# Decode attention with an MLP gate on one core: first and last loads cut by partitions, 96 rows of w2 moved to ACT's DMA queue

## The chip, the core and the metric

One core of a Trainium2 chip runs the whole kernel. The metric is device microseconds for one execution; less is better. Times given as a median come from runs without the profiler; everything else comes from one execution under the hardware profiler, whose own time is given beside its span below.

## The reference

Two tokens (B = 2, one position each, D = 512). With `xn = layernorm(x)`:

```
q = (xn @ wq) as (B, 32 heads, 1, 128)
s = softmax(q . k_cache * 128**-0.5) . v_cache      # 8192 positions a head
s = s as (B, 1, 4096) @ wo
g = silu( gelu( layernorm(xn) @ w1 + b1 ) @ w2 + b2 )   # w1 (512, 1376), w2 (1376, 512)
out = x + s * g
```

All is float32. k_cache and v_cache have 268 MB each, wq and wo 8.4 MB each, w1 and w2 2.8 MB each.

## The kernel before

The 64 (token, head) pairs are worked off in N = 32 steps of two heads. In a step, partition p holds 64 positions of one head: a K tile is 128 partitions x 64 KB (8.4 MB), a V tile the same. There are two K buffers (`kpool`) and one V buffer (`vpool`).

- **Loads.** All large loads go through `load` (L60) and SyncE's queue, in program order. `load_k(n + 2)` stands at the end of step n, after the last reader of K tile n; `load_v(n)` stands in step n behind `weighted(n - 1)`, the last reader of the only V buffer. A load waits on SyncE until its buffer is free, and what stands behind it in SyncE's queue waits with it. Each DMA has one of eight completion semaphores in turn, and a DMA also waits until the earlier DMA with its semaphore has landed.
- **Start.** The MLP's weights and small tensors lie in `boot`, which takes the place of the V buffer; wq takes one of the K buffers. SyncE issues w1 (L98), the first 1280 rows of w2 (L99), w2's last 96 rows (L100), wq (L101) and K tile 0 in two halves. ScalarE (ACT) issues x (L96), b1 in two loads (L107, L108) and b2 (L109) on its own queue. Then layernorm twice (`layernorm`, L152 to L158), transposes (L165), `mlp` (L196: w1, then b1 at L202, gelu, L215: w2, L218: b2), q (`project_q`, L241; `gather_q`, L251; `queries`, L262). TensorE runs these in that order. Only then can VectorE begin step 0 (L279), SyncE issue K tile 1 (waits for L241, the last reader of wq) and V tile 0 (waits for the last reader of `boot`).
- **A step.** VectorE multiplies K by q in two halves (L279) and sums over the 128 elements (L284), takes maxima (L288, L297); ACT does exp (L312); TensorE does the weighted sum over V (`weighted`, L327) and gathers the result (L337, L350). `max_dve(n - 1)` and `exps(n - 1)` stand in step n, after its first multiplication; `weighted(n - 1)` and `load_v(n)` follow.
- **End.** The last V tile is loaded in five pieces (`PIECES`, in 128ths of a partition's positions), wo in five (`WO_PIECES`, in its 32 rows c of 128 partitions x 2 KB) into a freed K buffer. At the end, 8 matmul instructions a row c (L419) sum `on` times wo, and two VectorE operations (L423, L424) and two small DMAs (L427) finish.

Of the kernel before, what the change touches and what calls it, by code (L numbers as in the profile page):

```python
# [8 lines left out]
F32 = mybir.dt.float32  # L9
AF = mybir.ActivationFunctionType  # L10
# [3 lines left out]
EPS = 1e-5  # L14
# [5 lines left out]
def decode_kernel(ctx: ExitStack, tc: tile.TileContext, x, kc, vc, wq, wo, w1, b1, w2, b2, out):  # L20
    nc = tc.nc
    P = 128
    B, H, S, DH = kc.shape
# [15 lines left out]
    NF = F // P  # L39
    FT = F - NF * P  # L40
    PH = P // H
    OC = DH // PH
    ZP = P - U * PH

    consts = ctx.enter_context(tc.tile_pool(name="consts", bufs=1))
    kpool = ctx.enter_context(tc.tile_pool(name="kpool", bufs=2))
    vpool = ctx.enter_context(tc.tile_pool(name="vpool", bufs=1))
    small = ctx.enter_context(tc.tile_pool(name="small", bufs=2))
# [9 lines left out]
    def load(dst, src, cuts):  # L58
        for a, e in zip(cuts, cuts[1:]):
            nc.sync.dma_start(dst[:, a:e], src[:, a:e])  # L60
# [5 lines left out]
    def load_v(n, cuts=(0, KP), pool=vpool, tag="v"):  # L66
        V[n] = pool.tile([P, KP, DH], F32, tag=tag, name=f"v{n}")
        load(V[n], vf[n], cuts)


    PIECES = (0, 32, 64, 96, 112, 128)
    WO_PIECES = (0, 8, 16, 24, 30, 32)


    wq_sb = kpool.tile([P, ND, H * DH], F32, tag="k", name="wq_sb")
# [3 lines left out]
    def take(p, n):  # L79
        a = used[0]  # L80
        used[0] += n
        assert used[0] <= KP * DH
        return boot[:p, a:a + n]

    w1_sb = take(P, ND * F).rearrange("p (c f) -> p c f", f=F)
    w2_sb = take(P, (NF + 1) * D).rearrange("p (c n) -> p c n", n=D)
    x_sb = take(B, D)
# [5 lines left out]
    z = take(P, P)  # L93
    th = take(P, P)

    nc.scalar.dma_start(x_sb, x.rearrange("b s d -> (b s) d"))  # L96

    nc.sync.dma_start(w1_sb, w1.rearrange("(p c) f -> p c f", p=P))  # L98
    nc.sync.dma_start(w2_sb[:, :NF, :], w2[:NF * P, :].rearrange("(p c) n -> p c n", p=P))  # L99
    nc.sync.dma_start(w2_sb[:FT, NF, :], w2[NF * P:, :])  # L100
    nc.sync.dma_start(wq_sb, wq.rearrange("(p c) n -> p c n", p=P))  # L101
    load_k(0, (0, KP // 2, KP))


    b1_sb = consts.tile([P, NF + 1], F32, name="b1_sb")
    nc.vector.memset(b1_sb, 0.0)
    nc.scalar.dma_start(b1_sb[:, :NF], b1[:NF * P].rearrange("(p c) -> p c", p=P))  # L107
    nc.scalar.dma_start(b1_sb[:FT, NF:NF + 1], b1[NF * P:, None])  # L108
    nc.scalar.dma_start(b2_sb, b2[None, :])  # L109
# [5 lines left out]
    nc.vector.memset(ones, 1.0)  # L115
    srow = consts.tile([1, HP], F32, name="srow")
    nc.vector.memset(srow, SCALE)
    eps_t = consts.tile([B, 1], F32, name="eps_t")
    nc.vector.memset(eps_t, EPS)

    mod = consts.tile([P, R], F32, name="mod")

# [231 lines left out]
    for n in range(N):  # L354
# [11 lines left out]
        if 1 <= n < LATE - 1 or n >= LATE:  # L366
# [7 lines left out]
            elif n == N - 1:  # L374
                load_v(N - 1, PIECES)
        if n >= LATE:
# [22 lines left out]
            load_v(n)  # L399

    wo_sb = kpool.tile([P, OC, D], F32, tag="k", name="wo_sb")
    load(wo_sb, wo.rearrange("(p c) n -> p c n", p=P), WO_PIECES)

    n = N - 1
    max_dve(n)
# [49 lines left out]
```

## Time and profile before

| | us |
|---|---|
| median of 3 runs (1307.24 to 1308.63) | 1308.48 |
| the profiled execution, its own time | 1307.31 |
| span of its trace, first to last instruction | 1305.5 |
| VectorE busy | 1128.8 (86%) |
| TensorE matmul busy | 444.4 (34%) |
| ACT busy | 84.0 (6%) |
| DMA queue q1 (SyncE's), share of 16 DMA engines | 99.3% |

The share of a DMA queue is the time that its packets took, over 16 engines for the whole span. A busy VectorE does not say that VectorE sets the end: the chain of waits from the last instruction backwards passes through DMA for 50% of the span and through VectorE for 48%.

### The profile page before, as it was taken

The page shows a single profiled execution, that of the slowest core. Times are in us where ns is not written, and L with a number is a line of the kernel's source. Part 1 is how long each engine was busy: PE and PEld are TensorE (multiplying, and loading weights), DVE is VectorE, ACT ScalarE, POOL GpSimd, SP SyncE. Part 2 cuts the span into 40 slices and gives each one's busy share as a digit, 9 for nine tenths or more (in the row PEclk, how much of TensorE's full clock was granted, in tenths as well). Part 3 has the DMA queues.
Part 4 walks back from the last instruction along what each step waited for, and adds up shares of the span by engine and source line. Part 5 has one row for each costly group of instructions (what it writes and reads, how often), then busy time and mean ns, then how long its engine had stood idle before and what let it go on. Part 6 is the DMA issues. An engine that isn't in the chain of part 4 may idle for free.

```text
span 1305.5 us, 7374 instructions
## 1 busy us (share of the span) xinstructions
PE 444.4 (34%) x3258; PEld 173.2 (13%) x3258; DVE 1128.8 (86%) x261; ACT 84.0 (6%) x276; POOL 2.8 (0%) x12
## 2 busy tenths in 40 slices
PE   6403333322333322333322333331333332231266
PEld 6101111111111101111100101110111101110013
DVE  1499989888889988889988888988888988889980
ACT  1100000000000000000000000000000000000000
POOL 0000000000000000000000000000000000000000
PEclk9756666556666656666655666655666655665668
DMA  9999999999999999999999999999999999999998
GB/s 398 440 424 442 424 442 422 442 424 442 424 442 424 438 430 436 432 434 432 432 436 428 440 426 438 428 440 424 440 426 440 424 444 422 446 404 426 438 416 339
DMA packets 11509, 559.76 MB, mean 429 GB/s; under 512 B 1515, under 2 KB 1523, under 8 KB 1750
## 3 DMA queue, kind: packets, MB, share of 16 engines
q1 hardware_dynamic: 11208, 559.29, 99.3%
q8 instruction: 25, 0.41, 0.1%
q10 hardware_dynamic: 270, 0.01, 0.0%
q14 instruction: 6, 0.05, 0.0%
HBM read 559.30 MB, written 0.00 MB: 428 GB/s over the span
## 4 chain that ended last, share of the span: by engine, by line
DMA 50%; DVE 48%; PE 1%; ACT 0%; issue 0%; SPq 0%; DVEq 0%
DMA k<-in_A_k_cache_dram 45%; DVE k L279 24%; DVE sc L284 24%; DMA wq_sb<-in_A_wq_dram 3%; DMA wo_sb<-in_A_wo_dram 2%; PE pq L241 1%; DVE nm L297 0%; ACT boot L244 0%; PE acc L419 0%; PE pqa L251 0%; SPq L60 0%; PE pb L262 0%; DVE mx L288 0%; SPq L100 0%; SPq L99 0%
## 5 line engine op out<-in xcount | busy, mean ns | idle before, releaser
L279 DVE TENSOR_TENSOR k<-k,q 128x8192 f32<-128x8192 f32 x64 | 555.5, 8681 | 109.7 <-DMA k<-in_A_k_cache_dram 98.0
L284 DVE TENSOR_REDUCE sc<-k 128x64 f32<-128x8192 f32 x64 | 552.4, 8666 | 0.0
L327 PE MATMUL po<-v,pz 128*8 128x512 f32 x2048 | 295.6, 742 | 202.3 <-DMA v<-in_A_v_cache_dram 202.3
L305 PE MATMUL pn<-nm,srow 1*64 1x1 f32 x128 | 11.7, 246 | 336.4 <-DVE nm L297 336.4
L327 PEld LDWEIGHTS po<-v,pz 128*8 128x8 f32 x2048 | 57.2, 104 | 422.8 <-DMA v<-in_A_v_cache_dram 213.7
L292 PE MATMUL pm<-ident,mx 128*1 128x128 f32 x32 | 11.8, 369 | 222.0 <-DVE Z L342 164.2
L305 PEld LDWEIGHTS pn<-nm,srow 1*64 1x64 f32 x128 | 9.0, 193 | 340.6 <-DVE nm L297 340.5
L334 ACT COPY o<-po 128x512 f32<-128x512 f32 x32 | 18.8, 586 | 516.3 <-PE po L327 516.3
L307 ACT COPY bias<-pn 128x1 f32<-128x1 f32 x32 | 5.1, 160 | 583.2 <-PE pn L305 583.2
L337 PE MATMUL pt<-mod,o 128*128 128x2 f32 x256 | 33.7, 254 | 22.9 <-ACT o L334 22.9
L337 PEld LDWEIGHTS pt<-mod,o 128*128 128x128 f32 x256 | 31.0, 191 | 52.6 <-ACT o L334 52.6
L318 PE MATMUL OA<-ones,ZR 128*128 128x1 f32 x64 | 18.6, 359 | 51.8 <-ACT ZR L315 51.8
L292 PEld LDWEIGHTS pm<-ident,mx 128*1 128x1 f32 x32 | 2.5, 79 | 224.4 <-issue 189.2
L312 ACT ACTIVATE pz<-sc,bias 64x128 f32<-64x128 f32 x64 | 25.5, 399 | 1.4
L318 PEld LDWEIGHTS OA<-ones,ZR 128*128 128x128 f32 x64 | 15.8, 307 | 54.5 <-ACT ZR L315 54.5
L262 PE MATMUL pb<-q_all,ident 64*64 64x128 f32 x128 | 21.6, 438 | 0.3 <-ACT q_all L253 0.3
L342 DVE TENSOR_TENSOR Z<-blk,pt 128x8 f32<-128x8 f32 x32 | 4.9, 152 | 18.4 <-PE pt L337 18.4
L196 PE MATMUL ph<-yT,boot 128*128 128x2 f32 (+1 forms) x88 | 19.5, 359 | 0.8 <-DMA boot<-in_B_w_dram 0.8
L196 PEld LDWEIGHTS ph<-yT,boot 128*128 128x128 f32 (+1 forms) x88 | 19.4, 317 | 0.9 <-ACT yT L166 0.9
L202 DVE TENSOR_TENSOR gh<-ph,b_sb 128x22 f32<-128x22 f32 x1 | 0.2, 181 | 21.0 <-PE ph L196 21.0
L350 PE MATMUL OA<-mod,Z 128*128 128x32 f32 x64 | 15.3, 332 | 4.4 <-DVE Z L342 4.3
L350 PEld LDWEIGHTS OA<-mod,Z 128*128 128x128 f32 x64 | 15.7, 304 | 4.8 <-DVE Z L342 4.8
(81 smaller groups left out, 119.5 us busy)
## 6 DMA issues: line engine op xcount, KB each, us to landing
k<-in_A_k_cache_dram SPq DMA_DIRECT2D x2, 4096.0 KB, 46.9
v<-in_A_v_cache_dram SPq DMA_DIRECT2D x3, 2048.0 KB, 19.2
wo_sb<-in_A_wo_dram SPq DMA_DIRECT2D x3, 2048.0 KB, 22.1
boot<-in_B_w_dram SPq DMA_DIRECT2D x1, 2752.0 KB, 9.7
boot<-in_B_w_dram SPq DMA_DIRECT2D x1, 2560.0 KB, 15.9
v<-in_A_v_cache_dram SPq DMA_DIRECT2D x2, 1024.0 KB
wo_sb<-in_A_wo_dram SPq DMA_DIRECT2D x1, 1536.0 KB
wo_sb<-in_A_wo_dram SPq DMA_DIRECT2D x1, 512.0 KB, 29.5
```

Of the source, the lines that this page charges most:

```text
L196: nc.tensor.matmul(ph[:w.shape[1], f * B:(f + 1) * B], w, yT[:, c, :], start=(c == 0), stop=(c == ND - 1))
L262: nc.tensor.matmul(p[HP * s:HP * (s + 1), :], w, q_all, start=True, stop=True)
L279: nc.vector.tensor_tensor(out=k, in0=k, in1=qb, op=ALU.mult)
L284: nc.vector.tensor_reduce(out=SC[n][:, a:e], in_=K[n][:, a:e, :], axis=AX.X, op=ALU.add)
L292: nc.tensor.transpose(p[:1, :], MX[n], ident)
L305: nc.tensor.matmul(p[HP * s:HP * (s + 1), :1], srow, nm[:, s:s + 1], start=True, stop=True)
L312: nc.scalar.activation(PZ[n % 3][r, :, s, :], sc[r], AF.Exp, bias=bias[r], scale=SCALE, accum_out=rs[r])
L318: nc.tensor.matmul(OA[:, b, OC:], ZR[:, a:a + P], ones[:, :1], start=False, stop=False)
L327: nc.tensor.matmul(po[R * j:R * j + U * JW, :], pz[:, t].rearrange("p s j -> p (s j)"), v[:, t * JW:(t + 1) * JW, :].rearrange("p j d -> p ...
L334: nc.scalar.copy(o4, PO[n % 2])
L337: nc.tensor.matmul(PT[n][:, :U], o4[:, i * DH:(i + 1) * DH], mod[:, i:U * JW:JW], start=(i == 0), stop=(i == JW - 1))
L350: nc.tensor.matmul(OA[:, b, :OC], Z[:, a:a + P], mod, start=False, stop=(n == N - 1))
```

## The change

- w1 is loaded in two DMAs instead of one: partitions 0 to 15, then 16 to 127.
- w2's last 96 rows go over ACT's queue instead of SyncE's, directly behind x.
- ACT first runs a `Sqrt` on a constant (`warm`), and only then issues x, w2's last rows, b1 and b2. The memset of that constant moves to the head of VectorE's stream.
- The last V tile is loaded in two pieces instead of five.
- wo is loaded in pieces of 16, 10, 4 and 1 rows, and its last row in four DMAs by partitions: 4, 5, 7 and 112.

```diff
-    PIECES = (0, 32, 64, 96, 112, 128)
-    WO_PIECES = (0, 8, 16, 24, 30, 32)
+    PIECES = (0, 64, 128)
+    WO_PIECES = (0, 16, 26, 30, 31, 32)
+
+    WO_SPLIT = (0, 4, 9, 16, 128)
...
-    nc.scalar.dma_start(x_sb, x.rearrange("b s d -> (b s) d"))
-
-    nc.sync.dma_start(w1_sb, w1.rearrange("(p c) f -> p c f", p=P))
+    w1_v = w1.rearrange("(p c) f -> p c f", p=P)
+    for p0, p1 in ((0, 16), (16, P)):
+        nc.sync.dma_start(w1_sb[p0:p1], w1_v[p0:p1])
     nc.sync.dma_start(w2_sb[:, :NF, :], w2[:NF * P, :].rearrange("(p c) n -> p c n", p=P))
-    nc.sync.dma_start(w2_sb[:FT, NF, :], w2[NF * P:, :])
     nc.sync.dma_start(wq_sb, wq.rearrange("(p c) n -> p c n", p=P))
     load_k(0, (0, KP // 2, KP))
...
+    eps_t = consts.tile([B, 1], F32, name="eps_t")
+    nc.vector.memset(eps_t, EPS)
     b1_sb = consts.tile([P, NF + 1], F32, name="b1_sb")
     nc.vector.memset(b1_sb, 0.0)
+    warm = small.tile([B, 1], F32, tag="warm", name="warm", bufs=1)
+    nc.scalar.activation(warm, eps_t, AF.Sqrt)
+    nc.scalar.dma_start(x_sb, x.rearrange("b s d -> (b s) d"))
+    nc.scalar.dma_start(w2_sb[:FT, NF, :], w2[NF * P:, :])
     nc.scalar.dma_start(b1_sb[:, :NF], b1[:NF * P].rearrange("(p c) -> p c", p=P))
...
-    eps_t = consts.tile([B, 1], F32, name="eps_t")
-    nc.vector.memset(eps_t, EPS)
...
-    load(wo_sb, wo.rearrange("(p c) n -> p c n", p=P), WO_PIECES)
+    wo_v = wo.rearrange("(p c) n -> p c n", p=P)
+    load(wo_sb, wo_v, WO_PIECES[:-1])
+    for p0, p1 in zip(WO_SPLIT, WO_SPLIT[1:]):
+        nc.sync.dma_start(wo_sb[p0:p1, OC - 1], wo_v[p0:p1, OC - 1])
```

## The prediction

> **What bounds the kernel now.** I read first the page's DMA rows and its 40 slices, then the chain of waits at its end, then the timelines of the first 160 us and the last 10.
>
> ```profile
> DMA  9999999999999999999999999999999999999998
> GB/s 398 440 424 442 424 442 422 442 424 442 424 442 424 438 430 436 432 434 432 432 436 428 440 426 438 428 440 424 440 426 440 424 444 422 446 404 426 438 416 339
> ...
> q1 hardware_dynamic: 11208, 559.29, 99.3%
> ...
> q10 hardware_dynamic: 270, 0.01, 0.0%
> ```
>
> Every slice has busy DMA engines, and q1, SyncE's queue, fills 99.3% of them. So the DMA queue is the bound, although the chain puts half of the span on VectorE: it follows each K load back to the VectorE sum that freed its buffer, but K tile 3, issued at 119.21, lands 35.4 us later, and 8.4 MB take 19.4, so it stood 16 us in the queue. The time is then start of the first packet (1.75 us), bytes over rate, any gap in which the queue runs dry, and what follows the last byte. Only the first and last slices (398, 339 GB/s) leave something to gain. The end, in the timeline:
>
> ```profile
> 1296.12 1.93 PE L419 MATMUL acc<-wo_sb,on 128*2 128x128 f32 x64 [2.16 <-DMA wo_sb<-in_A_wo_dram]
> ...
> 1299.80 1.93 PE L419 MATMUL acc<-wo_sb,on 128*2 128x128 f32 x64 [1.75 <-DMA wo_sb<-in_A_wo_dram]
> 1301.80 0.29 DVE L423 TENSOR_TENSOR res<-acc,gate 128x128 f32<-128x128 f32 x1 [12.84 <-PE acc L419]
> ```
>
> Rows 24 to 31 of wo begin when rows 24 to 29 have landed (1299.76 by the trace's landing events); the last two rows land at 1301.0, just as TensorE gets to them, and it ends at 1301.73. The start, in the same view:
>
> ```profile
> 0.74 0.39 SPq L98 DMA_DIRECT2D boot<-in_B_w_dram  x1
> 0.74 0.54 ACTq L96 DMA_DIRECT2D boot<-in_A_x_dram  x1
> ...
> 1.33 0.37 ACTq L107 DMA_DIRECT2D b_sb<-in_B_b_dram  x1
> ...
> 4.29 1.28 ACT L156 ACT_TABLE_LOAD   x1
> ...
> 10.53 19.49 PE L196 MATMUL ph<-yT,boot 128*128 128x2 f32 x88 [0.84 <-DMA boot<-in_B_w_dram]
> 30.06 0.18 DVE L202 TENSOR_TENSOR gh<-ph,b_sb 128x22 f32<-128x22 f32 x1 [20.97 <-PE ph L196]
> ...
> 38.03 7.05 PE L241 MATMUL pq<-wq_sb,xnT 128*2 128x512 f32 x64 [1.48 <-DMA wq_sb<-in_A_wq_dram]
> ```
>
> b1 is wanted at 30.06, and TensorE has 1.48 us to spare before wq. These two decide below.
>
> **Part by part.**
>
> *End.* The piece with rows 26 to 29 ends where the old fourth piece did, 1299.76. TensorE does 32 instructions (1.93 us / 64 = 0.030 each, 0.97) to 1300.77, row 30 (lands about 1300.4) to 1301.0, and row 31 from its landing: 8 instructions, 7 x 0.026 + 0.27 for the last = 0.45, to 1301.5, so 0.23 sooner. The last row now waits for four semaphores: one wait on TensorE's sequencer took 0.05 (row of L419), up to 0.15. The split by partitions shifts one 2 KB row (0.08 us in the packets of w2's last rows) off most DMA engines and up to two onto four of them: -0.08 to +0.16 on the last landing. The end takes -0.15, bounds -0.3 and +0.2. The other new pieces lie in cover: the second half of V is wanted after 32 of 64 matmuls, at about 1282.0, and lands at 1281.4; rows 0 to 15 of wo land at 1291.2, are done (4.95) at 1296.2, and rows 16 to 25 land only then, at about 1297.3. Without that cover nothing is late by over 1 us. SyncE's last three DMAs wait for V landings (the last at 1281.4, by the changed program's semaphores), 18 us before their bytes are due.
>
> *First load.* In the packet records the 16 engines begin their first 22,016-byte row between 1.75 and 2.72 and need 1.52 us on the mean, 0.82 for later ones. If one row an engine makes all begin together, at most 0.28 + 0.70 = 0.98 is gained; if the latency is HBM's, nothing; a second DMA's issue (0.39) might leave a hole, +0.3. I take -0.3, nearer to nothing, as even the row that began last took 0.98.
> [...]
>
> *w2's last rows.* On q1 their 96 packets of 2 KB and the first wq packets behind them (2.75 us on the mean, later 2.42) cost about 0.9 + 0.33 us an engine, where the bytes alone need 0.45. Between w1's big packets they should cost 0.08 each, 0.5 in all: -0.5, bounds 0 and -0.7.
>
> *Table load.* It moves from 4.29 to the start; x is issued after 1.28 + 0.29, at about 2.35 instead of 0.74. Behind it ACT issues w2's rows, b1 and b2 (0.4 each), to 4.7.
>
> *The new wait.* ACT's queue q10 is served one packet, or one semaphore write, after each q1 packet on the same engine: b1's 40-byte packets stand in the records exactly at the ends of w1's packets, 0.82 us apart. And b1, issued at 1.33, got its first turn at 5.64, after four w1 rows. So turns are the currency. Per engine q10 now has 6 + 1 (w2's rows), 8 + 1 (b1), 6 + 1 (b1's tail) = 23 turns, two more on the engines with x. w2's rows arrive at about 3.9, during row 2 of w1, and by the same delay are served after row 5, at 6.55. From there q1 offers 4 packets of w1 and a semaphore, 8 + 1 of w2, 8 + 1 of wq: 23, the last at about 36.3, since a wq packet takes 2.42. With x's two turns, up to two half-size K packets (1.21) more: b1's tail lands between 37.4 and 38.6 (landing events come 0.45 after), not at 17.4. VectorE's L202 waits for it: 30.06 becomes about 38, L215 1.77 later, its 4.37 and L218's 0.40 end at 44.5, and L241 starts there instead of 38.03: delay D = 6.0 to 7.2, I take 6.6. b2 lands by 41, before L218. x lands at about 7.5, so L196 starts near 12.7 and ends near 32: covered by b1. Were q10 served at once, this cover would go and L196 still leave L241 within 1 us of its time.
>
> What does D cost? All of step 0 moves by D, and these issues with it:
>
> ```profile
> 84.31 0.33 SPq L60 DMA_DIRECT2D k<-in_A_k_cache_dram  x1
> ...
> 105.59 0.33 SPq L60 DMA_DIRECT2D v<-in_A_v_cache_dram  x1
> 119.21 0.33 SPq L60 DMA_DIRECT2D k<-in_A_k_cache_dram  x1
> ```
>
> A DMA needs 1.0 from issue to first packet (0.74 to 1.75) and some 0.9 more before it streams. K tile 1 (45.13) must stream when K tile 0 ends on the engines, 55.1 to 56.9: room for D = 8.1. K tile 2 (84.31) follows V tile 0, from 93.8: 7.6. V tile 1 (105.59) follows K tile 2, 113.2 to 115.5: room 5.7 on the earliest engine, 8.0 on the latest, 6.7 on the mean; 0.8 less, as the gains above bring the queue forward. K tile 3 (119.21, room 11) and all later ones have more. So D = 6.6 costs the mean engine 0.7, the latest nothing: I take +0.5, bounds 0 and +3.5 (two turns more).
>
> Sum: -0.15 - 0.3 - 0.5 + 0.5 = -0.45. Against the profiled time 1306.9; the median is 1.17 above that execution, so 1308.0.
>
> **The rivals.**
>
> *The delay is absorbed.* If q10 is served soon after its arrival, because b1's wait for four rows had another cause (DMAs issued just before it), w2's rows get three turns more and b1's tail lands by 33: D under 3, no gap: -0.95, 1307.5. For it: only one such delay is in the trace. Against it: the same delay on all 16 engines.
> [...] The records here show one 40-byte descriptor a turn.
>
> *The queue runs dry (slower).* Place: V tile 1 behind K tile 2. Price: 1 us for each us of D beyond 5.9. Two more turns lost, through a later x or an HBM stall, give D = 9.0, a loss of 3.1, and 1308.48 - 0.95 + 3.1 = 1310.6; from D = 9.5 it is slower by over 0.2%. For it: no cover but the queue's backlog, and wq packets make a lost turn cost 2.42. Against it: my count puts only the last turn into that region.
>
> *The engines' spread closes (faster).* The last engine lands at 1301.0, the mean of the 16 at 1299.6. If split and pieces took all 1.4 and the first load its 0.98: -0.3 - 1.4 - 0.98 - 0.5 = -3.2, 1305.3. Against it: the split moves 0.08 to 0.16 us.
>
> *It does nothing.* Both start gains are HBM latency that stays: 1308.5.
>
> **Numbers.** Forecast 0.50, absorbed 0.25, runs dry 0.11, spread closes 0.07, nothing 0.07. A change under 0.2% (2.6 us) can't be told from none here. Same: 0.50 + 0.25 + 0.07 = 0.82; slower 0.11; faster 0.07. The range runs from near the faster case, 1305.7, to the dry queue at D = 9.0, 1310.6.
>
> **What would show it.** x's BN statistics at 7 us or later, L202 near 38 released by the b1 DMA, L241 at 43 to 46, V tile 1 issued at 111 to 113; wq's first packets at 2.42; TensorE's last row from 1301. Wrong if L202 stays near 32 (turns miscounted) or the DMA share dips between 113 and 117 by more than 1 us.

## The result, and the profile after

| | before | after |
|---|---|---|
| median, 6 runs each in one comparison | 1307.62 us (1307.11 to 1308.63) | 1312.61 us (1311.93 to 1313.38) |
| ratio, 95% interval | | 1.0036 (1.0024 to 1.0048) |
| the profiled execution | 1307.31 | 1313.38 |
| its span | 1305.5 | 1311.5 |

The change costs 5.0 us by the medians. My range ended at 1310.6. The page of the changed kernel, against the lines shown of before:

```profile
DMA  9999999999999999999999999999999999999997
GB/s 333 444 420 430 434 438 427 436 428 436 434 434 434 432 434 430 436 428 436 430 436 432 436 433 428 438 424 444 424 440 430 432 434 432 436 414 420 436 427 322
...
q1 hardware_dynamic: 10696, 559.09, 99.2%
...
q10 hardware_dynamic: 382, 0.21, 0.1%
```

The DMA engines are as busy as before in every slice but the last (the rows of nines; 7 for 8 at the end), but the first slice moved 333 GB/s in place of 398: 65 GB/s over 32.8 us is 2.1 MB, or 4.9 us at 433 GB/s (the rate of a K tile, 8.4 MB in 19.4 us). The windows view of the first stretches shows it closer; its last three columns are TensorE's granted clock, the DMA share and GB/s. First before, then after:

```profile
4.00:8.00 4.00, 0.64 (x4) 0.55 (x4) 1.94 (x6) 1.89 (x4) 0.00 (x0) 1.00 1.03 441
8.00:12.00 4.00, 2.10 (x11) 2.05 (x11) 0.76 (x3) 1.75 (x4) 0.00 (x0) 1.00 1.00 422
```

```profile
4.00:8.00 4.00, 0.68 (x9) 0.22 (x9) 1.68 (x5) 0.45 (x2) 0.00 (x0) 1.00 1.02 236
8.00:12.00 4.00, 1.19 (x8) 1.01 (x8) 1.87 (x7) 1.37 (x4) 0.00 (x0) 1.00 0.98 271
```

About the same DMA share (1.02 and 0.98 for 1.03 and 1.00), but only 54% and 64% of the bytes: here a busy share says that packets are under way, not how many bytes move. In the packet records w1's rows, 22,016 bytes each, take 1.51 us on the mean, against 0.91, and w1's last row ends at 15.1 instead of 10.0. The timeline of the changed kernel (line numbers are its own: from the MLP on 7 to 10 higher than before's, x's load is L114 for L96, `load` is still L60):

```profile
0.74 1.28 ACT L113 ACT_TABLE_LOAD   x1 [0.74 <-PEq L451]
...
0.89 0.54 ACTq L114 DMA_DIRECT2D boot<-in_A_x_dram  x1
...
16.20 19.49 PE L203 MATMUL ph<-yT,boot 128*128 128x2 f32 x88 [5.29 <-DMA boot<-in_B_w_dram]
42.87 0.18 DVE L209 TENSOR_TENSOR gh<-ph,b_sb 128x22 f32<-128x22 f32 x1 [32.56 <-DMA b_sb<-in_B_b_dram]
...
49.94 7.05 PE L248 MATMUL pq<-wq_sb,xnT 128*2 128x512 f32 x64
...
116.93 0.33 SPq L60 DMA_DIRECT2D v<-in_A_v_cache_dram  x1
```

Two delays lie on one another: w1 is waited for until 16.2 (was 10.5), and b1 until 42.87 (was wanted at 30.06). A ledger from the packet records tells which of them the end sees: the time at which a given number of MB had moved, less the same time before.

| MB moved | 8 | 21 | 47 | 55 | 200 | 500 | 559 |
|---|---|---|---|---|---|---|---|
| after | +4.9 | +4.9 | +4.9 | +5.6 | +5.1 | +5.1 | +5.4 |

All but a part of 1 us is there when w1 and w2 have landed. The second step, between 47 and 55 MB, is V tile 1, issued at 116.93, behind K tile 2.

### The profile page after: what moved, and what is told of

Its sections match the earlier page's. It is cut to its first block, busy times and chain, and to the rows that moved or that the text cites. A ratio compares the mean times of both kernels' runs of the same rounds, so it can differ in the third digit from the quotient of the medians.

```text
span 1311.5 us, 7378 instructions
## 1 busy us (share of the span) xinstructions
PE 444.4 (34%) x3258; PEld 173.5 (13%) x3258; DVE 1128.7 (86%) x261; ACT 82.7 (6%) x276; POOL 2.8 (0%) x12
## 4 chain that ended last, share of the span: by engine, by line
DVE 50%; DMA 45%; PE 3%; issue 1%; ACT 0%; SPq 0%; DVEq 0%
DMA k<-in_A_k_cache_dram 42%; DVE k L286 25%; DVE sc L291 25%; DMA wo_sb<-in_A_wo_dram 2%; PE ph L203 1%; DMA boot<-in_B_w_dram 1%; PE pq L248 1%; PE pgate L222 0%; DVE nm L304 0%; ACT boot L251 0%; PE acc L429 0%; SPq L60 0%; PE pqa L258 0%; DVE Z L349 0%; DVE mx L295 0%
## 5 line engine op out<-in xcount | busy, mean ns | idle before, releaser
L203 PEld LDWEIGHTS ph<-yT,boot 128*128 128x128 f32 (+1 forms) x88 | 19.4, 317 | 5.3 <-issue 5.3
```

What stands on the lines that cost most here:

```text
L203: nc.tensor.matmul(ph[:w.shape[1], f * B:(f + 1) * B], w, yT[:, c, :], start=(c == 0), stop=(c == ND - 1))
```

## The experiments

Theory P: w1's cut by partitions makes its rows slow. Rival T: the turns on ACT's queue, which I had foreseen, cost the 5 us. The first four runs undo or do one part alone.

**w1 in one DMA, all else as changed.**

```diff
-    for p0, p1 in ((0, 16), (16, P)):
-        nc.sync.dma_start(w1_sb[p0:p1], w1_v[p0:p1])
+    nc.sync.dma_start(w1_sb, w1_v)
```

> The changed kernel with w1 loaded in one DMA of 128 partitions again; all else as changed. Theory P (loading w1 by partitions makes its rows slow: they took 1.51 us on the mean in the changed kernel, 0.91 before): w1's rows are back at about 0.9, the start comes 5 us sooner, VectorE's first use of b1 falls from 42.9 to about 38, and the time from 1312.6 to about 1308. Rival T (the loss is the turns that b1 waits for on ACT's queue, and the dry DMA queue behind them; w1's rows do not matter for the end): the time stays within 1 us of 1312.6. Rival S (what slows w1 is the x and w2 traffic of ACT's queue beside it): w1's rows stay near 1.5.

1308.41 us, ratio to before 1.0004 (0.9995 to 1.0014); rows 0.94 us. P holds, and S falls, since ACT's traffic still stands beside these rows. What is left is T by itself, and its chain is as predicted:

```profile
38.11 0.18 DVE L208 TENSOR_TENSOR gh<-ph,b_sb 128x22 f32<-128x22 f32 x1 [28.32 <-DMA b_sb<-in_B_b_dram]
44.86 7.05 PE L247 MATMUL pq<-wq_sb,xnT 128*2 128x512 f32 x64
...
113.33 0.33 SPq L60 DMA_DIRECT2D v<-in_A_v_cache_dram  x1
```

L247 is 6.83 late (44.86 against 38.03). The queue does run dry before V tile 1 streams. The windows view, before, then this run:

```profile
108.00:120.00 12.00, 0.35 (x3) 0.38 (x3) 11.97 (x5) 0.00 (x0) 0.00 (x0) 0.61 1.01 437
```

```profile
108.00:120.00 12.00, 6.32 (x52) 1.93 (x44) 12.00 (x3) 0.59 (x1) 0.00 (x0) 0.78 0.91 362
```

437 less 362 GB/s over 12 us is 2.1 us at full rate. The ledger of this run agrees: 0.0 at 47 MB, +2.1 at 55, +2.0 at 559. Its profiled execution, 1309.55, is the highest of its ten runs; the median is only 0.7 above before, so the gap is not that large in every execution.

**w1's cut alone, in the kernel before.**

```diff
-    nc.sync.dma_start(w1_sb, w1.rearrange("(p c) f -> p c f", p=P))
+    for p0, p1 in ((0, 16), (16, P)):
+        nc.sync.dma_start(w1_sb[p0:p1], w1_v[p0:p1])
```

> The kernel before with only w1's load cut into partitions 0 to 15 and 16 to 127. Theory P: the rows take 1.5 us, w1 lands about 5 us later (15 instead of 10), wq and every later load with it, and the time is 1312 to 1313. Rival T: w1 lands later or not, but the time stays at 1307.6 within 1 us. Rival S: the rows take 0.9 and the time is 1307.6.

1312.76 us, ratio 1.0041 (1.0028 to 1.0055): the whole loss, from this edit alone. Ledger +5.2 from 8 MB to the end (5.1 to 5.3); rows 1.52 us. The first stretches move about as few bytes as in the changed kernel (236 and 271 GB/s):

```profile
4.00:8.00 4.00, 0.64 (x4) 0.55 (x4) 1.94 (x6) 1.89 (x4) 0.00 (x0) 1.00 0.96 226
8.00:12.00 4.00, 0.64 (x4) 0.55 (x4) 0.76 (x3) 1.75 (x4) 0.00 (x0) 1.00 0.94 254
```

T is refuted as the cause of the 5 us.

**w1 cut inside the partitions.**

```diff
+    for c0, c1 in ((0, 1), (1, ND)):
+        nc.sync.dma_start(w1_sb[:, c0:c1], w1_v[:, c0:c1])
```

> The kernel before with w1 in two DMAs as well, but cut inside the partitions (a quarter of each row, then three quarters), both over all 128 partitions. Theory P: full rate, the time within 1.5 us of 1307.6. Rival theory 'two DMAs in place of one' (the cut itself costs, wherever it lies): w1 lands 3 to 5 us later and the time is 1311 to 1313.

1307.77 us, ratio 1.0003 (0.9994 to 1.0012). The second DMA costs nothing that shows; what costs is the cut by partitions.

**The end alone.** The new `PIECES`, `WO_PIECES` and `WO_SPLIT`, in the kernel before.

> The kernel before with only the end changed: V in two pieces, wo in pieces of 16, 10, 4, 1 and its last row by partitions in 4, 5, 7, 112. My forecast's term: -0.15 us (-0.3 to +0.2). Theory P carried over to wo's last row: its 2 KB packets take 0.11 to 0.12 us instead of 0.08 (as in the changed kernel's trace), 8 of them, so the last landing comes 0.2 to 0.5 later and the time is 0 to +0.5. Neither theory allows +1 or more; the changed kernel's end, which came 6.0 us later than before where its start came 5.0 later, would then be the end's own loss.

1307.43 us, ratio 0.9999 (0.9990 to 1.0008): no difference to be told.

**Destination or source?** When 16 engines move 16 rows at a time, both ends lie close together. Four kernels load w1 in eight DMAs of 16 rows and cross the two:

```diff
+    for i in range(8):
+        nc.sync.dma_start(w1_sb[16 * i:16 * i + 16], w1_v[16 * i:16 * i + 16])    # f1
+        nc.sync.dma_start(w1_sb[16 * i:16 * i + 16], w1_v[i::8])                  # f2
+        nc.sync.dma_start(w1_sb[i::8], w1_v[16 * i:16 * i + 16])                  # f3
+        nc.sync.dma_start(w1_sb[i::8], w1_v[i::8])                                # f4
```

> The kernel before with w1 in eight DMAs of 16 rows: DMA i loads source rows 16i to 16i+15 into partitions 16i to 16i+15 (one row an engine, as in the changed kernel's first load). First of four that cross 'destination near or spread' with 'source near or spread'. Theory D (destination: the 16 partitions written at one time lie close together): rows take about 2.0 us, as the changed kernel's first 16 did. Theory H (source: HBM rows read at one time lie close together): also about 2.0. [...]

> As f1_near_near, but DMA i loads source rows i, i+8, i+16 ... (176 KB apart) into partitions 16i to 16i+15; w1's rows so lie on other partitions than the computation wants, which changes the MLP's values and nothing of the timing. Theory D: still about 2.0 us a row. Theory H: 0.8 to 0.9.

> As f1_near_near, but DMA i loads source rows 16i to 16i+15 into partitions i, i+8, i+16 ...; w1's rows so lie on other partitions than the computation wants. Theory D: 0.8 to 1.1 us a row. Theory H: about 2.0. [...]

> As f1_near_near, but DMA i loads source rows i, i+8, i+16 ... into partitions i, i+8, i+16 ... . Theories D and H both: 0.8 to 1.1 us a row. A third theory, that any DMA of 16 rows is slow (one row an engine, whatever the addresses), has about 2.0 in all four.

Mean us of a row, last three DMAs, where the queue is full:

| destination | source rows neighbouring | source rows 8 apart |
|---|---|---|
| 16 neighbouring partitions | 2.96 | 2.87 |
| partitions 8 apart | 1.69 | 1.69 |

Theory D has the order right and H falls: the source makes at most 0.09 us of difference, the destination 1.2 to 1.3. (The whole times, 1324.3, 1324.6, 1317.7 and 1316.7, one execution each, also hold waits of the later loads for the eight semaphores: in f1 SyncE issued w2 at 15.99, before at 1.19.) D's sizes were too low. The 2.0 us for neighbouring partitions held for the first of the eight DMAs alone (2.00 and 2.08), and in place of 0.8 to 1.1 the spread destination took 1.69, 2.1 times the full rate's 0.82.

**Closeness or few rows?**

```diff
+        r = slice(32 * (i // 2) + i % 2, 32 * (i // 2) + 32, 2)
+        nc.sync.dma_start(w1_sb[r], w1_v[r])                       # f5, eight DMAs
...
+    for p0, p1 in ((0, 64), (64, P)):                              # f6
```

> The kernel before with w1 in eight DMAs of 16 rows, partitions 0, 2, ... 30, then 1, 3, ... 31, then 32, 34, ... and so on, rows to their own partitions. With 16 neighbouring partitions a row took 2.97 us in the steady part, with partitions 8 apart 1.69. [...] Rival (what counts is how close together the 16 partitions lie): between the two, 2.0 to 2.97.

> The kernel before with w1 in two DMAs of 64 partitions, 0 to 63 and 64 to 127. [...] Rival (only loads that are no multiple of 32 partitions, or of few rows, are slow): 0.82 to 0.9 a row and 1307.5.

f5: 1.72 us a row, though its 16 partitions lie within 31. f6: 1.70, and 1314.44 us (one execution), so few rows are not the reason either. Closeness falls. Of the loads of 16 and 64 partitions, 16 neighbours take 2.9 to 3.0 us a row and the other three patterns (16 partitions 2 apart, 16 partitions 8 apart, 64 in one DMA) 1.7, against 0.82 for 128 partitions in one DMA. What in a pattern sets the rate is not shown, and no run loads these rows over fewer than 128 partitions at 0.82, so it is not shown either whether such a load could reach it.

**Turns on ACT's queue.** Two variants of the first run, w1 whole:

```diff
-    nc.scalar.dma_start(w2_sb[:FT, NF, :], w2[NF * P:, :])
...
     nc.scalar.dma_start(b2_sb, b2[None, :])
+    nc.scalar.dma_start(w2_sb[:FT, NF, :], w2[NF * P:, :])    # g1
```

> e1_w1_whole (the changed kernel with w1 in one DMA) with ACT's queue in another order: x, b1, b1's tail, b2, and only then w2's last rows. Theory T (one packet of ACT's queue per packet of SyncE's on each DMA engine): b1 and its tail need 16 turns (18 on two engines) in place of 23 (25), so VectorE's first use of b1 falls from 38.1 to the end of w1's matmuls, about 31; w2's rows take the last turns and land at 36 to 38; q's projection starts at 38 to 39 instead of 44.9, V tile 1 is issued at 106 to 108 instead of 113.3, and the DMA queue no longer runs dry between 111 and 119, where it lost 1.9 us of full rate in e1. Time 1.0 to 2.5 below e1's, so 1306 to 1307.4. Rival (b1's small packets themselves are late whatever stands ahead of them, for example because ACT issues them later): the first use of b1 stays at 36 to 38 and the time at 1308.4.

> e1_w1_whole with w2's last rows back on SyncE's queue, so ACT issues x, b1, b1's tail and b2 behind the early table load. Theory T: first use of b1 at about 31, V tile 1 issued at 105 to 107, no dry queue; my forecast's gain for w2's rows (-0.5) goes, wq's first packets are at 2.75 again instead of 2.43: 1306.5 to 1308. Rival (what delays b1 is the table load ahead of it on ACT, not w2's rows): the first use of b1 stays at 36 to 38.

g1, then g2, which issues those rows from SyncE ahead of wq as before did:

```profile
29.71 0.18 DVE L208 TENSOR_TENSOR gh<-ph,b_sb 128x22 f32<-128x22 f32 x1 [20.42 <-PE ph L202]
39.14 9.39 PE L247 MATMUL pq<-wq_sb,xnT 128*2 128x512 f32 x64
...
109.74 0.33 SPq L60 DMA_DIRECT2D v<-in_A_v_cache_dram  x1
```

```profile
30.11 0.18 DVE L208 TENSOR_TENSOR gh<-ph,b_sb 128x22 f32<-128x22 f32 x1 [20.42 <-PE ph L202]
38.23 7.05 PE L247 MATMUL pq<-wq_sb,xnT 128*2 128x512 f32 x64 [0.92 <-DMA wq_sb<-in_A_wq_dram]
```

In both, L208 follows w1's matmuls again, and V tile 1 streams without a gap (from 108 to 120, 438 GB/s in g1 and 437 in g2). T's account of the turns is right, and the early table load does not delay the first use of b1. g1 takes 1307.61 us, ratio 1.0001 (0.9992 to 1.0010); g2 1307.29, ratio 0.9997 (0.9988 to 1.0006). g1 is 0.8 below e1's median, not the 1.0 to 2.5 expected, and their intervals overlap, so the price of the dry queue shows in the traces and not in these times. V tile 1 was issued in g1 at 109.74, later than the 106 to 108 expected: q's projection took 9.39 in place of 7.05 and `weighted` 9.7 in place of 8.9. Neither beats before by what can be measured.

**Why the 112 rows are slow too.** Of the 5 us, the 16-row load carries the smaller part. In the changed kernel an engine's row of that load takes 0.5 us more than its first row before (2.05 against 1.52); the next row, the first of the 112-row load, takes 1.2 more (2.02 against 0.83), and the six behind it, at 1.1 to 1.4 us each, 3.1 together.

```diff
-    for p0, p1 in ((0, 16), (16, P)):
+    for p0, p1 in ((0, 112), (112, P)):    # h1
+    for p0, p1 in ((0, 96), (96, P)):      # h2
+    for p0, p1 in ((16, P), (0, 16)):      # h3
```

> The kernel before with w1 in partitions 0 to 111, then 112 to 127. What the 112-row load does by itself, from partition 0 and with nothing slow before it. [...] Rival A (the 112 rows of the changed kernel were slow in the wake of the 16-row load): 0.82 to 0.9.

> The kernel before with w1 in partitions 0 to 95, then 96 to 127. [...] Rival A: 0.82 to 0.9 in the first. [...]

> The kernel before with the changed kernel's two pieces of w1 in the other order: partitions 16 to 127, then 0 to 15. [...] Rival A: 0.82 to 0.9 for the 112.

Without each engine's first row, the 112 rows take 1.26 us on the mean in h1 and 1.31 in h3 (1.33 in the changed kernel), the 96 rows 1.58 in h2. The small loads behind them take 2.5 us for the 16 rows in h3 and 1.7 for h2's 32. The whole times, one execution each, are 1313.5 (h1), 1313.7 (h2) and 1314.5 (h3). Rival A, which had 0.82 to 0.9, falls: the wake of the small load is not needed. P holds, and in these loads 64 partitions (1.70) are slower than 96 (1.58), 96 slower than 112 (1.26 to 1.33), and 112 slower than 128 (0.82). The records, followed on each engine from one packet's end to the next one's start, show all engines slowed alike (1.21 to 1.33 in h1, 1.53 to 1.60 in h2). Why the rows of a 112-row load are slow stays open.

## Why the prediction was wrong

- **First load, -0.3 with bounds -0.98 and +0.3: here it failed.** Measured: +4.9 in the changed kernel's ledger, +5.2 in e2. I looked for the cost of a cut at its beginning (latency, a hole between two DMAs) and took the rate of the rows from those of a 128-partition load, 0.82 us. They took 2.0 while the two DMAs met and 1.1 to 1.4 afterwards: the step that failed is the assumption that a load over fewer partitions keeps the full rate. Before has one such load on q1, w2's last 96 rows, which cost about 0.9 us where the bytes need 0.45 (by the mean end of w2's big packets and the mean start of wq's, 0.8); I put that down to small packets. Its 2 KB packets took 0.08 us at the median and 0.105 on the mean, so they showed no lasting slow rate as h2's 22,016-byte rows do; why the two differ stays open. (The mean start of the first rows is 2.06 in the records, so the prediction's 0.28 should be 0.31; nothing hangs on it.)
- **w2's rows, -0.5:** 0.0 in e1's ledger at 47 MB. wq's first packets did go to 2.43 us (2.75 before), but the engines began them 0.3 us later on the mean (16.58 against 16.28), and w1's last row had ended at 10.61 against 10.02. Beside w1 and w2, ACT's packets cost what they saved behind them.
- **End, -0.15:** e4's interval, -1.3 to +1.0 us, holds it and decides nothing. In the traces, VectorE's first operation of the end begins 1.06 us after wo's last packet in e4, 1.15 in the changed kernel and 1.24 before, so the shorter tail is there in these single executions, 0.1 to 0.2 us.
- **The new wait, D = 6.0 to 7.2:** right where w1 is whole. In e1 D is 6.83, and b1 was first used at 38.11, forecast about 38. In the changed kernel D is 11.9, 5.1 more than in e1, which differs from it by w1's cut alone; so the signs that I gave for q's projection (43 to 46) and V tile 1 (111 to 113) were passed there, at 49.94 and 116.93. One step was wrong and did no harm: ACT issued x at 0.89, not 2.35, since its DMAs did not wait for the table load (0.74 to 2.02); x's statistics ran at 5.34 in e1 and 5.88 in the changed kernel, where I had 7 or later.
- **Dry queue, +0.5:** +0.7 in the changed kernel, where w1's own lateness moved the queue back as well; +2.0 in e1's profiled execution. V tile 1 was issued 7.7 late there, 0.9 more than D, since `weighted(0)` took 9.89 instead of 8.94; my price, 1 us for each us beyond 5.9, makes 1.8 of that.
- **The rival 'the queue runs dry'** had the right sign and a time of 1310.6, but not the cause: in the changed kernel's ledger 0.7 of the 5 us is its. The 'absorbed' rival falls too: D was not under 3 but 6.83 in e1, and turns were lost, one packet a turn, as in the trace of before (b1's 40-byte packets 0.82 us apart, w1's row time).

## What to carry to other kernels

Do not cut a large load by partitions to let its first rows start sooner, which cost 5.2 us here (e2's ledger): cut it, if at all, along the bytes of each partition, over all 128, which cost nothing here (e3, ratio 1.0003). For wo's last row, 2 KB a partition, the cut by partitions made no difference that could be told (e4, ratio 0.9999). When a queue is to carry a transfer beside a saturated one, count turns, not bytes: in these traces it got one packet per packet of the other (b1's packets 0.82 us apart beside w1's rows before), so what is wanted first must be issued first, and what stood in line beside wq's 64 KB packets paid 2.4 us for each turn (the packets of b1's tail in the changed kernel stand 2.42 apart). The DMA engines' busy share did not show the slow load (1.02 for 1.03 from 4 to 8 us); GB/s did (236 for 441).

## What the runs showed of the hardware

A DMA of 22,016-byte rows, us of a row with the queue full, by the partitions that it fills: all 128, 0.82 (before); 112, 1.26 to 1.33 (h1, h3, the changed kernel); 96, 1.58 (h2); 64, 1.70 (f6); 16 partitions 2 or 8 apart, 1.7 (f5, f3, f4); 16 neighbours, 2.9 to 3.0 (f1, f2).

ACT's queue issued DMAs while a table load of 1.28 us ran on the engine: in the changed kernel x at 0.89 beside the load from 0.74. That came 0.15 us later than before (0.74), and x was served 1.6 us later in e1 (3.32 against 1.68), behind a first row of w1.
